# A third and a fourth pair of attention units as one group beside the first block of a fused attention and two-MLP kernel

## The chip, the cores and the metric

The kernel runs on one core of a Trainium2 chip. The metric is the device time in microseconds of one execution. Engines are named as the profile names them: PE (TensorE, matrix products), PEld (its weight loads), DVE (VectorE), ACT (ScalarE), POOL (GpSimd) and SP (the queue from which nearly all DMAs are issued).

## The reference

Local attention over 4 batches, 8 heads, 576 positions and head size 64 (window 32; in the upper four heads only every fourth position of a window of 128), then two MLPs over 2304 tokens with model width 512 and hidden width 2048, all in float32:

```
attn = softmax(where(mask, q @ k.T / sqrt(D), -1e9))
x = (attn @ v), heads side by side, as [2304, 512]
h = maximum(x @ w_in, 0);   x = (h * h) @ w_out        # first MLP
h = x @ w2_in;              out = (h * cos(h)) @ w2_out  # second MLP
```

## The kernel before, in words

The tokens are cut into five blocks of 512, 384, 512, 512 and 384 (`SIZES`). Each MLP goes through the blocks, and inside a block through 16 chunks of the hidden width. A chunk needs twelve matmuls in `product1` (L446, called h below: h9 is chunk 9 of block 0), elementwise work in `middle`, and twelve matmuls in `product2` (L499, called y), in two halves of six. Each product is made of three matmuls on operands that are split into a high and a low part, so every operand is split by ACT (high part) and DVE (low part) first. Weights are split by `split_w` (L144): DVE L152, L155, L158, ACT L161, DVE L163.

Attention is worked in units (one pair of heads, 192 positions). A number in `GROUPS` stands for two units, u and u+3, which here is called a pair. The first six pairs run before block 0. The later 18 are put beside the MLP by `group` (L386), in entries of one pair or of two. An entry of one or two pairs goes through these steps: scores on PE into two PSUM banks (L251); mask, maximum, exponential and normalisation on DVE and ACT (L398, L401, L335, L322, L323, L326); transposes on PE into one bank for each pair (L346) and ACT copies of them (L416); values on PE into two banks (L264); and `tokens_out` (L304), which drains these two banks: first every ACT copy (L313, the high part), then every DVE subtraction (L316, the low part), bank by bank, in as many pieces as the runs of tokens and the edges of blocks make.

The order of the work is written as events with a time. One unit of time is one hidden chunk, so block 0 is 0 to 16. In block 0, h of chunk fc stands at fc, and the two halves of y of chunk fc at fc + 2.5 and fc + 2.75. `PLACES` gives the time at which an entry's scores stand, and the values of the entry ahead of it stand 0.003 before that place, or 0.003 behind it where both entries hold one pair (`alone`, L604). Transposes come at the earlier of place + 1 + number of pairs and 0.5 before the next place (L605). The drain comes 0.12 behind the next place, or 0.42 where `alone` holds. Loads of queries and keys stand 1.5 before the place, loads of values 0.6 behind it.

From time 2.4 on each matmul is pinned behind the one written before it (`pe`, L207), so PE follows the order of the events exactly. For the other engines and for the loads the framework plans the order itself: the earliest event first among what is ready by its own costs.

Products h, scores, transposes and values all take their PSUM bank from one pool of four (`ps_h`, L105 and L212); the other four banks hold y. A buffer of the pool goes to its next user when the readers of the last one are done. Unit buffers in SBUF come from two rings of three, "uq" and "uv" (L188, L199); the second load of the second pair of an entry goes into the "uv" ring (L611).

```
        tr = min(t + 1 + len(us) + 0.5 * (i == 0), t2 - 0.5)
        in_steps([t, *soft, tr, later_by(tr, 0.1), t2 + (0.003 if alone else -0.003), later_by(t2, 0.42 if alone else 0.12)],
                 us, group, us)
```

Here t is the entry's place, t2 the next one, and soft holds the softmax steps, from 0.15 behind the place on.

Of the kernel before, what the change touches and what calls it, by code (L numbers as in the profile page):

```python
# [43 lines left out]
SQUARE_ON_ACT = (0, 4)  # L44
LAG = (2, 3)

GROUPS = ((12,), (13,), (18,), (19,), (20,), (14, 24), (30, 31), (32, 25), (26, 36), (42, 43), (44, 37), (38,))
PLACES = (3.74, 6.74, 8.74, 10.74, 12.74, 14.74, 22.49, 25.74, 28.74, 36.49, 42.74, 46.49, 51.74)
PINNED = (2.4, 96)


# [40 lines left out]
def attention_moe_moe(ctx: ExitStack, tc: tile.TileContext, units, windows, masks, w1, w2, out):  # L92
# [22 lines left out]
    def at(t, f, *a):  # L115
        events.append((t, len(events), f, a))
# [463 lines left out]
    at(before(49) - 1e-3, load_masks)  # L580
    place = PLACES
    with_weights = {us for us, t in zip(GROUPS, place) if t < NF}

# [14 lines left out]
    for t, n in MORE_FILL:  # L598
        at(before(t), fill_more, n)
    for i, us in enumerate(GROUPS):  # L600
        t, t2 = place[i:i + 2]
        by = lambda d: later_by(t, d)
        soft = [by(0.15)] + [by(d + a) for a in range(len(us)) for d in (0.75, 0.8)]
        alone = len(us) == 1 and len(GROUPS[min(i + 1, len(GROUPS) - 1)]) == 1  # L604
        tr = min(t + 1 + len(us) + 0.5 * (i == 0), t2 - 0.5)  # L605
# [148 lines left out]
```

## Time and profile before

| | |
|---|---|
| time, median of 3 runs | 859.26 us (859.16 to 860.20) |
| the profiled execution's own time | 859.97 us |
| its span, first to last instruction | 858.2 us |
| busy: PE, PEld, DVE, ACT, POOL | 850.1, 742.3, 499.1, 436.2, 52.8 us |
| mean granted TensorE clock | 0.999 |

Busy shares are means over the whole span. The matrix work of the two MLPs has the same shape from block to block, while the splitting of the first weights and the softmax of the later units lie in the first 130 us. What happens around the change is therefore read from the stretch of 70 to 130 us, in which block 0 ends.

### The profile page before, as it was taken

What the parts mean: (1) busy time and instruction counts of PE and PEld (TensorE: products, weight loads), DVE (VectorE), ACT (ScalarE), POOL (GpSimd) and SP (SyncE); (2) the same over time, 40 slices, a digit from 0 to 9 for tenths busy, and PEclk for the clock granted to TensorE, in tenths of its full rate; (3) what the DMA queues carried; (4) which work ended last, traced back from release to release, by engine and by line L of the source; (5) the groups of instructions that cost most, each with busy time, mean ns of one, the idle gap of its engine ahead of it and who ended that gap; (6) DMA issues with size and microseconds to landing.
All of it is one profiled execution on the core that took longest, in us unless ns stands there. A gap on an engine that the chain in (4) does not pass through costs nothing.

```text
span 858.2 us, 15509 instructions
## 1 busy us (share of the span) xinstructions
PE 850.1 (99%) x6251; PEld 742.3 (87%) x6251; DVE 499.1 (58%) x966; ACT 436.2 (51%) x1062; POOL 52.8 (6%) x86
## 2 busy tenths in 40 slices
PE   9899999999999999999999999999999999999998
PEld 5688889999888888889998888899988888888998
DVE  5999953464424342226999964556555555555554
ACT  6677873454424332225656654555544545445554
POOL 0000000000000000000002211111111111111110
PEclk9999999999999999999999999999999999999999
DMA  7867711240202020004565300010020002000101
GB/s 268 296 223 255 237 61 50 82 153 19 97 1 101 1 100 0 1 1 171 196 220 182 115 1 1 34 64 2 1 87 1 1 0 86 1 0 1 50 1 37
DMA packets 24663, 68.58 MB, mean 80 GB/s; under 512 B 2640, under 2 KB 8464, under 8 KB 24592
## 3 DMA queue, kind: packets, MB, share of 16 engines
q1 hardware_dynamic: 24432, 67.48, 22.8%
q8 instruction: 49, 0.80, 0.4%
q14 instruction: 22, 0.18, 0.1%
q10 hardware_dynamic: 160, 0.11, 0.0%
HBM read 58.15 MB, written 9.44 MB: 79 GB/s over the span
## 4 chain that ended last, share of the span: by engine, by line
PE 75%; DVE 10%; issue 8%; ACT 2%; DMA 2%; POOL 1%; SPq 0%; POOLq 0%; ACTq 0%; DVEq 0%
PE y L508 36%; PE h L452 35%; DVE wt L155 3%; DVE wt L158 2%; PE h L264 1%; DVE w L163 1%; DVE wt L152 1%; POOL kf L471 1%; DVE gl L494 1%; PE h L251 1%; DMA wraw<-w 1%; ACT early L335 1%; DMA early<-w 1%; PE h L346 1%; DMA xraw<-y 1%
## 5 line engine op out<-in xcount | busy, mean ns | idle before, releaser
L508 PE MATMUL y<-gh,w 128*128 128x512 f32 (+1 forms) x1280 | 397.1, 370 | 0.3 <-ACT o L526 0.3
L452 PE MATMUL h<-xh,w 128*128 128x512 f32 (+1 forms) x1280 | 393.2, 368 | 1.0 <-DVE w L163 1.0
L452 PEld LDWEIGHTS h<-xh,w 128*128 128x128 f32 x1280 | 237.4, 188 | 32.2 <-DVE w L163 1.4
L508 PEld LDWEIGHTS y<-gh,w 128*128 128x128 f32 x1280 | 237.6, 188 | 31.0 <-ACT o L526 0.6
L508 PE MATMUL y<-gl,w 128*128 128x512 f32 (+1 forms) x640 | 235.4, 368 | 0.2 <-DVE gl L494 0.2
L452 PE MATMUL h<-xl,w 128*128 128x512 f32 (+1 forms) x640 | 235.2, 367 | 0.0
L483 DVE TENSOR_TENSOR r<-h,r 128x512 f32<-128x512 f32 (+1 forms) x128 | 81.9, 640 | 168.6 <-ACT r L480 95.1
L494 DVE TENSOR_TENSOR gl<-r,gh 128x512 fp32r<-128x512 f32 (+1 forms) x160 | 101.9, 637 | 124.6 <-ACT gh L492 124.3
L492 ACT CAST gh<-r 128x512 fp32r<-128x512 f32 (+1 forms) x160 | 92.1, 576 | 89.7 <-PE y L508 74.6
L452 PEld LDWEIGHTS h<-xl,w 128*128 128x128 f32 x640 | 120.2, 188 | 15.3
L508 PEld LDWEIGHTS y<-gl,w 128*128 128x128 f32 x640 | 120.2, 188 | 15.0 <-DVE gl L494 0.6
L479 ACT ACTIVATE r<-r 128x512 f32<-128x512 f32 (+1 forms) x80 | 47.2, 590 | 142.1 <-DVE r L476 142.1
L471 POOL TENSOR_SCALAR kf<-kf 128x512 f32<-128x512 f32 (+1 forms) x80 | 52.1, 652 | 794.1 <-DVE wt L155 459.2
L464 ACT ACTIVATE r<-h 128x512 f32<-128x512 f32 (+1 forms) x80 | 44.2, 552 | 95.8 <-PE h L452 95.7
L470 ACT ACTIVATE kf<-h,magic 128x512 f32<-128x512 f32 (+1 forms) x80 | 51.0, 638 | 22.1 <-PE h L452 20.3
L480 ACT ACTIVATE r<-r,halfpi 128x512 f32<-128x512 f32 (+1 forms) x80 | 54.5, 681 | 2.5
L474 DVE SCALAR_TENSOR_TENSOR r<-kf,h 128x512 f32<-128x512 f32 (+1 forms) x80 | 50.0, 625 | 6.8 <-POOL kf L471 6.8
L476 DVE SCALAR_TENSOR_TENSOR r<-kf,r 128x512 f32<-128x512 f32 (+1 forms) x80 | 51.0, 638 | 2.4
L161 ACT CAST w<-wt 128x512 fp32r<-128x512 f32 x64 | 39.4, 620 | 24.1 <-DVE wt L158 24.1
L163 DVE TENSOR_TENSOR w<-wt,w 128x512 fp32r<-128x512 f32 x64 | 44.0, 694 | 4.0 <-ACT w L161 3.8
L335 ACT ACTIVATE p<-p,nm 128x64 f32<-128x64 f32 x108 | 36.2, 339 | 9.9 <-DVE nm L401 9.9
L155 DVE SCALAR_TENSOR_TENSOR wt<-wraw,wt 128x512 uint32<-128x512 uint32 x58 | 39.6, 686 | 0.7
(60 smaller groups left out, 392.9 us busy)
## 6 DMA issues: line engine op xcount, KB each, us to landing
wraw<-w SPq DMA_DIRECT2D x58, 512.0 KB, 4.0
uq<-units SPq DMA_DIRECT2D x36, 208.0 KB, 4.8
uv<-windows SPq DMA_DIRECT2D x18, 384.0 KB, 4.7
early<-w SPq DMA_DIRECT2D x6, 512.0 KB, 4.8
y<-o SPq DMA_DIRECT2D x6, 512.0 KB, 2.6
xraw<-y SPq DMA_DIRECT2D x6, 512.0 KB, 5.3
out<-o SPq DMA_DIRECT2D x6, 512.0 KB, 2.8
early<-units SPq DMA_DIRECT2D x6, 416.0 KB, 5.3
```

Source lines behind the costliest of these rows:

```text
L155: nc.vector.scalar_tensor_tensor(out=t, in0=high, scalar=0xC0000000, in1=t, op0=ALU.bitwise_and, op1=ALU.bitwise_or)
L163: nc.vector.tensor_tensor(out=lo, in0=f32(t), in1=f32(hi), op=ALU.subtract)
L452: pe(nc.tensor.matmul(h, w[:, c * P:(c + 1) * P], x[:, c, :], start=c == 0 and i == 0, stop=c == NC - 1 and i == 2))
L470: nc.scalar.activation(out=kf, in_=h, func=AF.Identity, bias=magic, scale=INV2PI)
L471: nc.gpsimd.tensor_scalar(out=kf, in0=kf, scalar1=-MAGIC, scalar2=1.0, op0=ALU.add, op1=ALU.mult)
L474: nc.vector.scalar_tensor_tensor(out=r, in0=kf, scalar=-C1, in1=h, op0=ALU.mult, op1=ALU.add)
L476: nc.vector.scalar_tensor_tensor(out=r, in0=kf, scalar=-C2, in1=r, op0=ALU.mult, op1=ALU.add)
L480: nc.scalar.activation(out=r, in_=r, func=AF.Sin, bias=halfpi, scale=-1.0)
L483: nc.vector.tensor_tensor(out=r, in0=h, in1=r, op=ALU.mult)
L492: nc.scalar.copy(out=gh, in_=r)
L494: nc.vector.tensor_tensor(out=gl, in0=r, in1=f32(gh), op=ALU.subtract)
L508: pe(nc.tensor.matmul(y[e], w[:, e * P:(e + 1) * P], g, start=fc == 0 and n == 0, stop=fc == NF - 1 and n == 2,))
```

## The change

```diff
-GROUPS = ((12,), (13,), (18,), (19,), (20,), (14, 24), (30, 31), (32, 25), (26, 36), (42, 43), (44, 37), (38,))
-PLACES = (3.74, 6.74, 8.74, 10.74, 12.74, 14.74, 22.49, 25.74, 28.74, 36.49, 42.74, 46.49, 51.74)
+GROUPS = ((12,), (13,), (18, 19), (20,), (14, 24), (30, 31), (32, 25), (26, 36), (42, 43), (44, 37), (38,))
+PLACES = (3.74, 6.74, 8.99, 11.99, 14.49, 22.49, 25.74, 28.74, 36.49, 42.74, 46.49, 51.74)
```

The entries (18,) and (19,), at 8.74 and 10.74, become one entry (18, 19) at 8.99. Entry (20,) goes from 12.74 to 11.99, and (14, 24) from 14.74 to 14.49. All else that hangs on places follows. The order on PE is now: transposes of 13 at 8.49; values of 13 at 8.987 and scores of 18 and 19 at 8.99; h9 at 9; transposes of 18 and 19 at 11.49; their values at 11.987 and scores of 20 at 11.99; h12 at 12; transposes of 20 at 13.99; its values at 14.487 and scores of 14 and 24 at 14.49. The drain of 13 goes from 9.16 to 9.11, that of 18 (and 19) to 12.11, that of 20 from 14.86 to 14.61. In the places before, at x.74, six matmuls of y stood between a place and the next h.

## Rows read from the trace of the kernel before

**Rows 1.** The page: busy time of the engine, share of the span.

```profile
...
PE 850.1 (99%) x6251; PEld 742.3 (87%) x6251; DVE 499.1 (58%) x966; ACT 436.2 (51%) x1062; POOL 52.8 (6%) x86
...
```

**Rows 2.** Waits of PE, 40 to 850 us: total, times, longest.

```profile
...
PE y L508 <- ACT o L526: 0.3, 1, 0.3
```

**Rows 3.** Waits of all engines, 60 to 126 us.

```profile
...
PEld h L452 <- DVE p L398: 0.5, 1, 0.5
...
```

**Rows 4.** Timeline of PE, 71 to 79 us: start, duration, line, count.

```profile
...
74.29 0.40 PE L508 MATMUL y<-gh,w 128*128 128x512 f32 x1
74.61 0.76 PE L251 MATMUL h<-uq 64*32 64x64 f32 x48
75.30 0.90 PE L264 MATMUL h<-pts,uv 64*64 64x32 f32 x48
76.13 0.50 PE L508 MATMUL y<-gh,w 128*128 128x512 f32 x1
76.46 0.40 PE L508 MATMUL y<-gl,w 128*128 128x512 f32 x1
...
77.39 0.40 PE L508 MATMUL y<-gh,w 128*128 128x512 f32 x1
77.84 0.50 PE L452 MATMUL h<-xh,w 128*128 128x512 f32 x1
...
```

**Rows 5.** Timeline of DVE, 75 to 100 us.

```profile
...
77.43 0.61 DVE L398 SCALAR_TENSOR_TENSOR p<-h,given 128x192 f32<-128x192 f32 x2
77.96 0.42 DVE L152 TENSOR_SCALAR wt<-wraw 128x512 uint32<-128x512 uint32 x1
78.30 0.55 DVE L401 TENSOR_REDUCE nm<-p 128x6 f32<-128x384 f32 x1
78.76 0.69 DVE L155 SCALAR_TENSOR_TENSOR wt<-wraw,wt 128x512 uint32<-128x512 uint32 x1
...
81.16 0.74 DVE L316 TENSOR_TENSOR xl<-h,xh 128x128 fp32r<-128x128 f32 x4
...
98.61 0.68 DVE L494 TENSOR_TENSOR gl<-r,gh 128x512 fp32r<-128x512 f32 x1
...
```

**Rows 6.** Timeline of PE, 112 to 123 us.

```profile
...
112.12 0.49 PE L346 MATMUL h<-ident,p 128*128 128x128 f32 x3
112.37 0.48 PE L508 MATMUL y<-gh,w 128*128 128x512 f32 x1
...
114.77 1.27 PE L251 MATMUL h<-uq 64*32 64x64 f32 x96
115.97 0.50 PE L508 MATMUL y<-gh,w 128*128 128x512 f32 x1
...
```

**Rows 7.** Timeline of PE, 130.9 to 133 us.

```profile
...
131.28 0.82 PE L346 MATMUL h<-ident,p 128*128 128x128 f32 x6
131.85 0.48 PE L508 MATMUL y<-gh,w 128*128 128x512 f32 x1
...
```

**Rows 8.** Timeline of PE, 168 to 174 us.

```profile
...
169.29 1.60 PE L264 MATMUL h<-p,uv 64*64 64x32 f32 x96
...
```

**Rows 9.** Timeline of ACT, 75 to 79 us; the brackets hold the idle time before and its releaser.

```profile
...
76.23 0.67 ACT L313 CAST xh<-h 128x128 fp32r<-128x128 f32 x4 [0.33 <-PE h L264]
...
```

**Rows 10.** Timeline of ACT, 111 to 119 us.

```profile
...
114.87 0.91 ACT L313 CAST xh<-h 128x48 fp32r<-128x48 f32 x6 [1.05 <-PE h L264]
...
```

**Rows 11.** Timeline of DVE, 112 to 120 us.

```profile
...
115.43 1.14 DVE L316 TENSOR_TENSOR xl<-h,xh 128x48 fp32r<-128x48 f32 x6 [2.61 <-ACT xh L313]
...
```

**Rows 12.** Timeline of ACT, 120 to 128 us.

```profile
...
125.76 1.54 ACT L326 ACTIVATE p<-p,rs 128x64 f32<-128x64 f32 x6
...
```

**Rows 13.** Timeline of the SP queue, 40 to 106 us: DMA issues.

```profile
...
78.86 0.33 SPq L202 DMA_DIRECT2D uv<-windows  x1
...
```

**Rows 14.** Timeline of PE, 29 to 33 us.

```profile
...
31.43 0.73 PE L452 MATMUL h<-xh,w 128*128 128x512 f32 x2 [0.96 <-DVE w L163]
...
```

**Rows 15.** Stretches: length, busy time of each engine, granted clock (PEclk), DMA share.

```profile
...
30.00:34.00 4.00, 3.04 (x13) 2.18 (x13) 3.90 (x11) 1.37 (x5) 0.00 (x0) 1.00 1.00 365
...
```

## The prediction

> **What bounds the kernel now.** I read the page first: PE is busy for 850.1 of 858.2 us [rows 1], so time is won or lost only where PE does more, does less, or stands still. Next the waits. From 40 us on PE has a single wait that counts as idle, 0.3 us [rows 2]; so a microsecond of stall that the change puts on PE is not won back later, as no later stall is there to shrink. Then the stretch of the change. The view of waits shows one that PE's busy time hides: PE's weight load for h waited for DVE's masking of scores, L398, for 0.5 us [rows 3]. On PE's timeline the last y before it starts at 77.39 and h9 at 77.84 [rows 4], 0.45 apart where two matmuls of this shape are 0.23 apart (76.46 to 77.39 are four steps). DVE's timeline says why: the first of the two L398 ends near 77.78 (start 77.43, half of 0.61 plus the overlap) [rows 5]. This is the bank pool at work: the scores of 18 and the values of 13 had taken all four banks, and h9 had to wait until one was read out. The last view is DVE itself: from 75 to 100 us it has no idle time worth naming, and the planner's order puts work behind work with earlier event times. The drain of 13 (event 9.16) ran at 81.16 [rows 5] though its ACT copies were done at 76.90 [rows 9]; splits and L494 with events up to 9.05 went first. Its neighbours 12, 18 and 19 were drained at the same point of the order.
>
> **What goes.** Attention costs PE its own time and a toll at each change of form: 0.09 going in (74.29 to 74.61 is 0.32, less 0.23) and 0.10 going out (76.13 to 76.46) [rows 4]. Scores of one pair take 0.69 and values 0.83 [rows 4]; scores of two pairs 1.20 [rows 6]; values of two pairs 1.53 (1.60 less the 0.07 by which the single one's duration passes its step) [rows 8]; transposes 0.25 for one pair [rows 6] and 0.57 for two [rows 7], with 0.08 going out in both.
>
> - Before, places 8.74 to 14.74: four tolls 0.76, scores 3 x 0.69 + 1.20 = 3.27, values 4 x 0.83 = 3.32, three transposes 3 x 0.33 = 0.99; sum 8.34.
> - After, places 8.99 to 14.49: three tolls 0.57, scores 1.20 + 0.69 + 1.20 = 3.09, values 0.83 + 1.53 + 0.83 = 3.19, transposes 0.65 + 0.33 = 0.98; sum 7.83.
>
> That saves 0.51. The stall of 77.84 goes too: 0.22 and the slow restart of 0.10, together 0.32. In all 0.83 less.
>
> **What comes: h9 directly behind the place.** Before, six y stood between a place and the next h. At 8.99 none does. Values of 13 and scores of 18 and 19 take all four banks, and h9 needs one at once. The first to come free is the first bank of the values, after two ACT copies and two DVE subtractions. Queued behind h9 on PE is everything, since matmuls are pinned.
>
> - PE: as before up to 74.29; then the second half of y, six steps of 0.23, and the toll: values from 75.98 to 76.81, scores to 78.01. Then h9 could start.
> - DVE: as before up to 77.43. From there to the drain at 81.16 it spent 3.73, of which L398 and L401 of the scores took 0.53 (77.43 to 77.96) and 0.46 (78.30 to 78.76) [rows 5]. These now have the event 9.14, behind the drain at 9.11, so they drop out: the drain starts at 77.43 + 2.74 = 80.17. Two of its four pieces are half of 0.74 [rows 5], so the bank is free at 80.55 and h9 starts at 80.6, after the 0.06 that lay between L398's end and h9 before.
>
> First stall: 80.6 - 78.0 = 2.6. From below 0: had DVE taken the two pieces when their copies end (76.9 plus half of 0.67 [rows 9], plus 0.4), the bank would be free at 77.7, ahead of PE. From above 3.8: two more split steps of 0.6 in front. I take 2.6, as the order of four drains out of four speaks for it.
>
> **The same at 11.99.** From h9 at 80.6 PE has six blocks of twelve matmuls (12 x 0.227 = 2.72), a restart of 0.10, transposes 0.65, and the toll: values of 18 and 19 from 97.8 to 99.3, scores of 20 to 100.0. Then h12 stands. The first bank holds six pieces now (18 and 19 follow one another in a dilated head, so their runs of tokens join: six, where three and four stood before). The copies start 0.1 behind the values, at 99.4, and six take 0.91 [rows 10], to 100.3; six subtractions take 1.14 [rows 11], to 101.4. DVE itself gets there in time: before, it needed 99.3 (98.61 + 0.68) - 81.16 = 18.1 from one drain to this point of the order [rows 5]; now one drain of 18 less (1.1) and its mask and maximum more (1.0), so it is there at about 98.2. Second stall 1.4. From below 0.5, if the subtractions run with the copies and scores cover a little more; from above 2.6, if DVE lags as at 8.99.
>
> A rule that speaks against the change is weighed here. The first subtraction of six pieces started at 115.43, 0.56 behind the first copy [rows 10, 11], which is about when the third copy, the last of its bank, ends. The Trainium skill, "PSUM — Partial Sum Buffer", section on bank collisions, says that two engines must not access one bank and quadrant at once, reads included, so copies and subtractions of one bank can only follow one another; by that rule the second stall stays at 1.4, and if piece followed piece it would be about 0.9. The row agrees with the rule.
>
> **What costs nothing, and its cover.** At 14.49 both halves of y of chunk 12 follow, 2.72 us, and scores 1.20, against a drain of about 2: no stall; DVE is idle 2.61 before that drain already [rows 11]. Were that cover gone it would cost as much as the second stall. The transposes of 18 and 19 at 11.49 need the last normalisation, L326. For the pair of pairs (14, 24) this ran at 125.76 to 127.30 [rows 12], 11.3 us behind the end of its scores at 115.97, with DVE free. Here there are 94.3 - 78.0 = 16.3 us, with DVE full; I take 0, bounded by 2. Loads: unit 22 goes into the "uv" ring at 7.79 and takes the third buffer, which is free from the start; 18's and 19's values then wait for the buffers of 12 and 13, the last free at 76.8; a load of values issued at 78.86 [rows 13] shows when such a buffer is taken again, and that is 19 us ahead of 97.8, when PE reads it. SP works in order, so such a load held up would hold weight loads behind it; as DVE never starves, up to 1 us, taken as 0. ACT and DVE lose two drain pieces each for good, beside PE: 0.
>
> **Sum.** -0.83 + 2.6 + 1.4 = +3.2. On the profiled execution, 859.97 (span 858.2 and 1.8 around it), that is 863.2. It stands 0.7 over the median, so the forecast by the median is 859.26 + 3.2 = 862.4.
>
> **Rivals.**
> 1. *No change: the drains are prompt.* If the planner puts the two subtractions of 13 where their copies end, the first stall is 0 and the second stays 0.5 to 1.4: -0.3 to +0.6, so 859.0 to 859.9. It decides from a first stall below 1.2 on. For it: L398 slipped between split steps at 77.43. Against: that had the earlier event; a drain never did so.
> 2. *Faster: h finds a bank.* If at one of the two places a bank outside the group's is free, both stalls go: 859.26 - 0.83 = 858.4. Against: four banks and four users.
> 3. *More stalls.* The last normalisation or SP's order delays the transposes by 1 to 2, or DVE lags at 11.99 too: 863.4 to 865. For it: DVE is full to 100 us.
> 4. *The clock falls.* PE stood still for 0.96 at 31.43 [rows 14] and the granted clock of 30 to 34 us stayed at 1.00 [rows 15]; 2.6 in one piece occurs in no stretch of this trace. If it fell from 2.4 to 1.2 GHz, the next twelve matmuls would take twice 2.72: +2.7, 865.1. The Trainium skill, "TensorE: Matmul & The Clock Gate", part 1, says that "the default state is throttled, and activity releases the throttle"; no row here shows the lower level after a pause.
>
> **How the numbers follow.** Forecast 57%, its own range 861.2 to 863.4; rival 1 21%, rival 2 5%, rival 3 12%, rival 4 5%. The range 859.5 to 864.4 leaves out rivals 2 and 4, half of rival 1 and the far end of rival 3. What a measurement can tell from no change is 0.2%, 1.7 us. Slower holds the forecast and rivals 3 and 4, less the forecast's low end where the first stall is half of what I take: 70%. Same holds rival 1 and that low end: 24%. Faster 6%.
>
> **What would show it.** PE (or PEld) h L452 waiting for DVE xl L316 twice, near 78 to 80.6 and 100 to 101.5; L316 starting near 80.2, right behind L494; L398 behind it; scores x96 between 76.8 and 78.0. No wait on L316, or two far below 1 us in sum, makes the forecast wrong; so does a wait at L346 for L326 larger than either.

## The result and the profile after

The changed kernel takes 866.60 us in the median of four runs (865.32 to 867.21), the kernel before 859.69 on the same chip: a ratio of 1.0077 (95% interval 1.0065 to 1.0089), 6.9 us slower. The forecast was slower by 3.2, with a range up to 864.4. The profiled execution took 867.21, with a span of 865.4 against 858.2.

The waits of PE over the whole execution (waiting engine, line, releaser: total, times, longest) hold the two waits that were forecast, and they are the largest:

```profile
PE h L452 <- DVE xl L316: 4.4, 2, 2.4
PE e L346 <- DVE xl L316: 1.7, 3, 0.8
```

PE's timeline around the first place, in the same columns as [rows 4]; the bracket holds the idle time and its releaser:

```profile
...
75.74 0.90 PE L264 MATMUL h<-pts,uv 64*64 64x32 f32 x48
76.57 1.49 PE L251 MATMUL h<-uq 64*32 64x64 f32 x96
80.49 0.47 PE L452 MATMUL h<-xh,w 128*128 128x512 f32 x1 [2.43 <-DVE xl L316]
...
81.72 0.63 PE L452 MATMUL h<-xl,w 128*128 128x512 f32 x1
...
84.91 0.40 PE L508 MATMUL y<-gh,w 128*128 128x512 f32 x1
```

By their length in [rows 6] the scores would end at 76.57 + 1.20 = 77.77, and h9 starts at 80.49: a stall of 2.7. The bracket has 2.43 of it, as the scores took 1.49 here in place of 1.27 [rows 6]; a short pause ahead of their last four matmuls, which comes back in the last section, changes nothing while h9 waits for the drain anyway. What is new stands behind the stall. From 81.72 on matmuls are 0.43 apart where they were 0.23 [rows 4], and h9's twelve take 4.42 to the first y at 84.91, where 2.82 was expected. The stretches (length, busy times, then the granted clock as the third value from the end) say why:

```profile
77.80:80.40 2.60, 0.26 (x5) 0.11 (x4) 2.60 (x7) 0.75 (x4) 0.00 (x0) 1.00 0.88 264
80.40:81.20 0.80, 0.71 (x3) 0.66 (x4) 0.80 (x5) 0.26 (x1) 0.00 (x0) 1.00 1.04 396
81.25:84.60 3.35, 3.35 (x9) 2.64 (x8) 3.35 (x8) 1.10 (x6) 0.00 (x0) 0.50 0.97 364
84.70:95.00 10.30, 10.30 (x47) 8.50 (x46) 8.09 (x18) 9.67 (x34) 0.00 (x0) 1.00 0.52 178
102.20:104.20 2.00, 0.05 (x4) 0.03 (x1) 2.00 (x10) 1.47 (x11) 0.00 (x0) 1.00 0.88 253
105.15:108.50 3.35, 3.35 (x9) 2.57 (x9) 3.28 (x8) 0.00 (x0) 0.00 (x0) 0.50 0.75 260
```

After each stall the granted clock is 0.50, 1.2 GHz in place of 2.4, for some eight or nine matmuls. While PE stood still DVE was busy without a break (2.60 of 2.60, 2.00 of 2.00), and its timeline around the first stall shows what it did, to be held against [rows 5]:

```profile
77.17 0.43 DVE L152 TENSOR_SCALAR wt<-wraw 128x512 uint32<-128x512 uint32 x1
77.51 0.69 DVE L494 TENSOR_TENSOR gl<-r,gh 128x512 fp32r<-128x512 f32 x1
78.11 0.69 DVE L155 SCALAR_TENSOR_TENSOR wt<-wraw,wt 128x512 uint32<-128x512 uint32 x1
78.72 0.69 DVE L163 TENSOR_TENSOR w<-wt,w 128x512 fp32r<-128x512 f32 x1
79.32 0.69 DVE L158 SCALAR_TENSOR_TENSOR wt<-wraw,wt 128x512 uint32<-128x512 uint32 x1
79.92 0.75 DVE L316 TENSOR_TENSOR xl<-h,xh 128x128 fp32r<-128x128 f32 x4
80.58 0.88 DVE L398 SCALAR_TENSOR_TENSOR p<-h,given 128x192 f32<-128x192 f32 x3
```

Five operations that nobody on PE was waiting for, then the drain, with the mask behind it. Around the second place, PE's timeline holds the second stall and a smaller wait ahead of it, in the six transposes, which took 0.57 in [rows 7]:

```profile
95.83 1.43 PE L346 MATMUL h<-ident,p 128*128 128x128 f32 x6
97.02 0.48 PE L508 MATMUL y<-gh,w 128*128 128x512 f32 x1
...
99.97 1.60 PE L264 MATMUL h<-p,uv 64*64 64x32 f32 x96
101.50 0.76 PE L251 MATMUL h<-uq 64*32 64x64 f32 x48
104.20 0.47 PE L452 MATMUL h<-xh,w 128*128 128x512 f32 x1 [1.95 <-DVE xl L316]
```

The transposes take 1.19, a wait of 0.6 for the last normalisation. DVE's load alone does not explain it. DVE stood idle for 2.1 ahead of 87.25, waiting for exponentials, and half of these ran on ACT behind L464, which waited 2.05 for the late and slow h9:

```profile
85.11 0.60 ACT L464 ACTIVATE r<-h 128x512 f32<-128x512 f32 x1 [2.05 <-PE h L452]
87.25 0.17 DVE L322 TENSOR_SCALAR rs<-sm 128x6 f32<-128x6 f32 x1 [2.12 <-ACT p L335]
```

Scores end at 102.19 and h12 starts at 104.20: a stall of 2.0. DVE and ACT between, which answer to [rows 10, 11]:

```profile
102.33 0.68 DVE L158 SCALAR_TENSOR_TENSOR wt<-wraw,wt 128x512 uint32<-128x512 uint32 x1
102.93 2.17 DVE L316 TENSOR_TENSOR xl<-h,xh 128x80 fp32r<-128x80 f32 x12
```

```profile
101.60 1.60 ACT L313 CAST xh<-h 128x80 fp32r<-128x80 f32 x12 [0.86 <-PE h L264]
```

Half of the twelve copies, those of the first bank, end about 102.5; DVE was then in a split step that the planner had put ahead, and began the drain at 102.93.

So the account is: PE's own time and the old stall -0.8, first stall +2.7, transposes +0.6, second stall +2.0, and twice 1.6 for the lower clock, +3.2: together +7.7, against 7.2 by the spans. PE reached the transposes of 13 at 72.56 in place of 72.71, which is 0.15 of the difference; and 0.2 is won back near 555 us, where the kernel before has its one wait of [rows 2] and the changed kernel has none.

### The profile page after: what moved, and what is told of

Same layout as the page of the kernel before. It is cut to its first block, busy times and chain, and to the rows that moved or that the text cites. A ratio compares the mean times of both kernels' runs of the same rounds, so it can differ in the third digit from the quotient of the medians.

```text
span 865.4 us, 15498 instructions
## 1 busy us (share of the span) xinstructions
PE 852.2 (98%) x6245; PEld 744.8 (86%) x6251; DVE 500.2 (58%) x964; ACT 435.4 (50%) x1060; POOL 52.8 (6%) x86
## 4 chain that ended last, share of the span: by engine, by line
PE 73%; DVE 12%; issue 9%; ACT 3%; DMA 2%; POOL 1%; SPq 0%; POOLq 0%; ACTq 0%; DVEq 0%
PE y L508 35%; PE h L452 35%; DVE wt L155 3%; DVE wt L158 2%; DVE w L163 2%; DVE wt L152 1%; PE h L264 1%; DVE gl L494 1%; POOL kf L471 1%; PE h L251 1%; ACT early L335 1%; DMA early<-w 1%; PE h L346 1%; DMA xraw<-y 1%; DVE xl L316 1%
## 5 line engine op out<-in xcount | busy, mean ns | idle before, releaser
L494 DVE TENSOR_TENSOR gl<-r,gh 128x512 fp32r<-128x512 f32 (+1 forms) x160 | 101.9, 637 | 124.5 <-ACT gh L492 124.1
L464 ACT ACTIVATE r<-h 128x512 f32<-128x512 f32 (+1 forms) x80 | 44.2, 552 | 104.5 <-PE h L452 104.4
```

The source lines that it names most:

```text
L494: nc.vector.tensor_tensor(out=gl, in0=r, in1=f32(gh), op=ALU.subtract)
```

## The experiments

Times are medians; each is set against the kernel before on the same chip in the same set of runs (859.96 in the first set of four, 859.87 in the second, 860.08 in the last two).

**Place moved back, grouping kept.** Is it the grouping or where it stands?

```diff
-PLACES = (3.74, 6.74, 8.99, 11.99, 14.49, ...
+PLACES = (3.74, 6.74, 8.74, 11.74, 14.49, ...
```

> The grouping of the change kept, the places moved back by 0.25 so that six y stand between place and next h (8.74, 11.74, 14.49). Theory (h waits for the first drained bank, and DVE takes the drain only at its event's turn): the drain's events are now 8.86 and 11.86, ahead of the splits at 8.93 to 9.05, so the stalls of h9 and h12 go to 0 to 0.3 each, the clock stays at 1.00, and the transposes at 11.24 may wait about 1 for the last normalisation: 859 to 861 us. Rival (a group of two pairs is itself too much beside block 0): 864 or more.

860.32, ratio 1.0001 (0.9992 to 1.0010). The waits on L316 shrink from 4.4 to one of 0.5, the transposes do not wait, the clock stays at 1.00. The grouping itself does no harm that can be told from noise. It does not win its 0.8 either: beside the 0.5 of that wait, a new pause of 0.6 stands behind the 144 small matmuls at the first place, one that is put down to no engine:

```profile
76.14 0.50 PE L508 MATMUL y<-gh,w 128*128 128x512 f32 x1
76.47 0.40 PE L508 MATMUL y<-gl,w 128*128 128x512 f32 x1
77.51 0.51 PE L508 MATMUL y<-gh,w 128*128 128x512 f32 x1 [0.64 <-issue]
```

**More cover at the second place.**

```diff
-PLACES = (3.74, 6.74, 8.99, 11.99, 14.49, ...
+PLACES = (3.74, 6.74, 8.74, 12.24, 14.74, ...
```

> The grouping kept, places 8.74, 12.24 and 14.74: six y behind the first place, twelve behind the second, transposes at 11.74. Theory: no stall at either h, a wait at the transposes of 0 to 0.6, clock 1.00: 858.7 to 859.8 us, the same as the kernel before or a little below (0.5 of PE's own time and the old 0.3 stall saved). Rival (the grouping costs): 862 or more.

860.23, ratio 1.0000 (0.9992 to 1.0009). No wait of PE on L316 or L326 is left from 70 us on, but the pause of 0.7 is there again, nearly as long as the saving. The time is 0.4 above the forecast range. What it is without the pause, the last experiment shows.

**The order of DVE alone.** PE's order is that of the changed kernel.

```diff
-        in_steps([t, *soft, tr, ..., later_by(t2, 0.42 if alone else 0.12)],
+        in_steps([t, *soft, tr, ..., later_by(t2, 0.42 if alone else 0.001 if t2 in (8.99, 11.99) else 0.12)],
```

> The change with its order on PE untouched; only the event of the two drains goes from 0.12 to 0.001 behind the place (8.991 and 11.991), ahead of the splits and L494 at 9.05 and 12.05 in DVE's order. Theory (the drain's turn on DVE sets the stall): first stall from 2.7 to about 0.9, second from 2.0 to about 1.2, so the clock falls at most once: 861 to 863.5 us. Rival (missing cover alone sets the stall, whatever DVE's order): 866.6 us as the changed kernel.

865.14, ratio 1.0053 (1.0040 to 1.0066). The first stall goes as forecast, from 2.7 to 0.9, with nothing changed but the drain's turn (the first bank's ACT copies were done before 77.4 in both kernels):

```profile
76.89 1.45 PE L251 MATMUL h<-uq 64*32 64x64 f32 x96
79.00 0.47 PE L452 MATMUL h<-xh,w 128*128 128x512 f32 x1 [0.66 <-DVE xl L316]
```

So missing cover alone does not set it; DVE's order does. Behind this shorter stall the clock stays at 1.00, and PE reaches the transposes 3.1 sooner than in the changed kernel. But 1.2 of that comes back at once, as the softmax is not ready:

```profile
92.71 0.49 PE L346 MATMUL h<-ident,p 128*128 128x128 f32 x3
94.01 0.33 PE L346 MATMUL h<-ident,p 128*128 128x128 f32 x1 [0.81 <-ACT p L326]
...
95.05 0.48 PE L508 MATMUL y<-gh,w 128*128 128x512 f32 x1
```

They take 2.34 in place of 1.19. The second stall did not shrink (2.4), against my 1.2, and the clock falls behind it: the first bank's copies were done near 100.5, yet DVE's drain came at 101.33, behind two more split steps. The forecast of 861 to 863.5 missed for these two reasons.

**The bank alone.** DVE's order at the first place and its number of operations are those of the changed kernel, but the two drains read the copied part in SBUF, so that the bank is free without DVE. The low part of the tokens of 13, 18 and 19 is left out (zero).

```diff
-            nc.vector.tensor_tensor(out=xl, in0=piece, in1=f32(xh), op=ALU.subtract)
+            nc.vector.tensor_tensor(out=xl, in0=f32(xh) if us in ((13,), (18, 19)) else piece, in1=f32(xh), op=ALU.subtract)
```

> The change with its order on PE and DVE; the subtractions of the two drains read the copied part in SBUF in place of the bank (the low part of these tokens is left out, it becomes zero), so that a bank is free when ACT's copies end, while DVE does as many operations as before. Theory (h waits for the bank that DVE has not read yet): first stall 0, second about 0.2, no fall of the clock behind them; DVE is as far behind as before, so the transposes of 18 and 19 wait 1.5 to 2.5 for the softmax: 860.5 to 863.5 us. Rival (h waits for DVE work in some other way, or missing cover alone sets it): 866 us, with the same two waits.

863.70, ratio 1.0037 (1.0024 to 1.0050). The drain still runs at 79.86, but h9 starts at 77.98, so it was the bank and nothing else of DVE's that h waited for:

```profile
77.98 0.50 PE L452 MATMUL h<-xh,w 128*128 128x512 f32 x1
79.86 0.76 DVE L316 TENSOR_TENSOR xl<-xh 128x128 fp32r<-128x128 f32 x4
```

The softmax is late instead (2.6 at the transposes), and h12 waits 0.3 for ACT's copies:

```profile
91.74 0.49 PE L346 MATMUL h<-ident,p 128*128 128x128 f32 x3
93.89 0.33 PE L346 MATMUL h<-ident,p 128*128 128x128 f32 x1 [1.66 <-ACT p L326]
...
94.93 0.47 PE L508 MATMUL y<-gh,w 128*128 128x512 f32 x1
```

The eight runs part by their mean granted clock: three at 0.999 or 1.000 took 860.95 to 861.52, five at 0.997 or 0.998 took 863.28 to 864.46. The trace is of one of the three (861.52); in the five the clock fell somewhere, against the forecast of no fall, and where is not known.

**One place at a time.**

```diff
-PLACES = (3.74, 6.74, 8.99, 11.99, 14.49, ...
+PLACES = (3.74, 6.74, 8.99, 12.24, 14.74, ...   # the first alone
+PLACES = (3.74, 6.74, 8.74, 11.99, 14.49, ...   # the second alone
```

> Grouping kept, only the first of the two bad places: 8.99, then 12.24 and 14.74 (twelve y behind the second). Theory (each place directly before an h costs its own stall and, behind it, a stretch at 1.2 GHz): first stall 2.7, one stretch of 3.4 us at the lower clock (about 1.6), no second stall, transposes with no wait; -0.8 + 2.7 + 1.6 - 0.3: 862.5 to 864 us. Rival (the loss comes from the second place, or only from both together): below 861 us.

> Grouping kept, only the second of the two bad places: 8.74, then 11.99 and 14.49. Theory: no wait for the drain at h9 (but the 0.8 us in which PE waits for nothing shown, as in the two kernels with 8.74), second stall about 2.0 to 3 (PE reaches it earlier, DVE does not), one stretch at the lower clock: 862.5 to 864.5 us. Rival (the first place alone makes the loss): 860 to 861 us.

863.02, ratio 1.0048 (1.0033 to 1.0062), and 863.32, ratio 1.0043 (1.0028 to 1.0058). Both lie inside their forecasts. Each has one wait on L316 (2.1 and 2.2 of idle time) and one stretch at the lower clock; the two excesses over the kernel before, 3.15 and 3.45, add up to 6.6, nearly the 6.9 of both.

**The place without the grouping.** The kernel before, with its single pairs:

```diff
-PLACES = (3.74, 6.74, 8.74, 10.74, 12.74, 14.74, ...
+PLACES = (3.74, 6.74, 8.99, 10.99, 12.99, 14.74, ...
```

> The grouping undone, the move kept: the five single pairs of the kernel before, with places 8.99, 10.99 and 12.99 directly before an h. Theory (the place, not the grouping): h9, h11 and h13 wait for the first bank that DVE reads, about 2.7, 1.5 to 2.5 and 0.5 to 1.5 us, with a stretch at the lower clock behind the longer ones: 865 to 870 us. Rival (the group of two pairs makes the loss): 859 to 861 us.

866.67, ratio 1.0080 (1.0065 to 1.0095): as bad as the change, with three places directly before an h where the change has two. Singles have their scores first, so h waits for the mask that reads the scores' bank, and the three waits sum to 3.9 with 2.9 the longest:

```profile
PE h L452 <- DVE p L398: 3.9, 3, 2.9
```

The time is inside the forecast, but not by its parts: the second and third wait are 0.8 and 0.2, below what was expected, and the clock falls once, for twice as long as in the changed kernel.

**PE kept at work in the stalls.** 11 and 8 matmuls with zero weights into a y bank, in the changed kernel, and then 11 in the kernel with the first place alone.

```diff
+    zero = const.tile([P, P], BF16, name="zero")
...
+    def keep_busy(n):
+        for _ in range(n):
+            pe(nc.tensor.matmul(ys[0, 0][0], zero, given[:, P:P + 512], start=False, stop=False))
...
+        nc.vector.memset(zero, 0.0)
...
+    at(8.995, keep_busy, 11)
+    at(11.995, keep_busy, 8)      # not in the second of the two kernels
```

> The change as it is, with 11 matmuls of zeros that add nothing to a y bank put ahead of h9 and 8 ahead of h12, so that PE works while it would stand still (about 2.4 and 1.7 us of stalls of 2.7 and 2.0). Theory (some 3 us of the loss are the lower clock that follows the two stalls): the granted clock stays at 1.00 and the time falls by about 3, to 863.0 to 864.0 us. Rival (the clock is a companion, the loss lies elsewhere): within 0.5 of the changed kernel's 866.6 us.

867.51 (866.20 to 871.83), ratio 1.0092 (1.0072 to 1.0113): neither forecast. The clock of the profiled execution (866.41) held at 1.00 through both places. From h9 to the transposes of (14, 24) PE took 54.55, where the changed kernel took 56.85, so 2.3 were saved by then (lines of this kernel stand five lower: L457 is h, L513 y, L321 the drain, L351 the transposes):

```profile
79.97 0.47 PE L457 MATMUL h<-xh,w 128*128 128x512 f32 x1
134.52 0.82 PE L351 MATMUL h<-ident,p 128*128 128x128 f32 x6
```

In the changed kernel the second of these is

```profile
137.34 0.82 PE L346 MATMUL h<-ident,p 128*128 128x128 f32 x6
```

Yet the time is no lower: near 194 and 235 us PE pauses 0.87 and 1.03 for "issue", in spots where the changed kernel does not. The wait for the drain at h12 is still there too, as the zeros cover only a part of it:

```profile
PE y L513 <- issue: 1.9, 2, 1.0
PE h L457 <- DVE xl L321: 1.4, 1, 1.4
```

> The kernel with only the first bad place (8.99, 12.24, 14.74), with the 11 matmuls of zeros ahead of h9. Theory (the stall makes the clock fall, and the stretch at 1.2 GHz costs 1.6 of the 3.2 us of this place): the granted clock stays at 1.00 behind the stall, h9 starts at the same time, and the time goes from 863.0 to 861.0 to 862.0 us, unless the 22 instructions more bring a new pause in which PE waits for nothing shown, as they did with both places. Rival (the clock costs nothing in the end, since DVE sets the pace to 100 us): 862.5 to 863.5 us.

862.69, ratio 1.0033 (1.0021 to 1.0044): inside the rival's forecast, not the theory's. The excess over the kernel before is 2.6, against 3.15 without the zeros, and the two intervals overlap. The clock held in the profiled execution, and the mean clock was 0.999 or 1.000 in seven of the eight runs, against 0.995 to 0.998 in all five without the zeros: it falls because PE stands still. What that saves, the traces show in part. From h9 to the transposes of (14, 24) the kernel with the zeros takes 53.13, the one without 54.00, which is 0.9 less of the 1.6 that the slow stretch takes:

```profile
81.40 0.58 PE L457 MATMUL h<-xh,w 128*128 128x512 f32 x1
134.53 0.82 PE L351 MATMUL h<-ident,p 128*128 128x128 f32 x6
```

```profile
80.34 0.47 PE L452 MATMUL h<-xh,w 128*128 128x512 f32 x1 [2.06 <-DVE xl L316]
134.34 0.81 PE L346 MATMUL h<-ident,p 128*128 128x128 f32 x6
```

But h9 starts 1.1 later here, and not at the same time as the theory wanted: PE was already behind by 0.4 at 40 us, and DVE comes to the drain 0.9 later. So this does not settle what a slow stretch costs in the end.

**Without the pause.** The kernel with 8.74, 12.24 and 14.74, with eight of the matmuls that warm PE early on left out:

```diff
-FILL = (7, 3, 2, 4, 4, 6)
-MORE_FILL = ((18.63, 3),)
+FILL = (7, 3, 2, 2, 2, 3)
+MORE_FILL = ((18.63, 2),)
```

> The kernel with places 8.74, 12.24 and 14.74 (860.2, as the kernel before), with eight warming matmuls fewer in the early part, so that PE's instruction stream stands 16 instructions earlier. Theory (the 0.8 us pause behind the 144 small matmuls at 8.74 is a fetch of instructions that was asked for inside them): the pause is gone, 859.3 to 859.7 us, a little under the kernel before. Rival (the pause belongs to the place itself, or the missing matmuls cost the clock early): 860 us or more.

860.46, ratio 1.0006 (0.9997 to 1.0015): the time is the rival's, though the pause behind the small matmuls is gone, as the theory had it. PE gets to h12 sooner and now waits there 0.56 for L316, and more goes at two waits of 0.3 and 0.6 near 470 and 555 us, for L494 and L526.

```profile
102.33 0.39 PE L508 MATMUL y<-gh,w 128*128 128x512 f32 x1
103.28 0.47 PE L452 MATMUL h<-xh,w 128*128 128x512 f32 x1 [0.56 <-DVE xl L316]
```

No version of the grouping beat the kernel before.

## Why the prediction was right and where it was wrong

- **What bounds, and that nothing wins time back later:** right for the whole (PE was 7.5 behind the kernel before at the end of block 0, and 7.2 at the end). Inside block 0 it was not: the DVE-bound part up to about 100 us gives a saved stall back at the next wait, as the drain's turn, the bank alone and the kernel without the pause showed.
- **h9 waits for the first drained bank, because of the drain's turn on DVE:** right. 2.7 for 2.6, the drain at 79.92 for 80.17, the mask behind it. That it is the bank, and that it is the turn, were each shown by changing that alone.
- **h12:** the mechanism right, the size 2.0 for 1.4. The term that failed is "DVE itself gets there in time": it did, but the planner had put split steps with later events ahead of it (it seems that by its own costs the copies were not done yet), and one of them held the drain 0.4 past their end. The Trainium skill, "PSUM — Partial Sum Buffer", section on bank collisions, says that two engines must not access one bank and quadrant at once, reads included. The changed kernel agrees where DVE was free: at 121.83 the first subtraction begins right behind the third copy, the last of its bank, which ends at 121.80.
- **Transposes at 11.49 at nothing:** 0.6, within the bound of 2. The margin left out ACT's turn: L464 waited for the late h9 with half of the exponentials behind it, and DVE, taken as full, stood idle for 2.1. With the 0.6 more at h12 this is rival 3 in small.
- **PE's own time:** right; values and scores of one pair take what the rows said, and so do the transposes where nothing holds them (0.57 with the places moved back).
- **The clock stays (rival 4, 5%):** this step failed and cost most of the miss. The chance was read from one pause of 0.96 [rows 14, 15], and a second fall was not thought of; the price of one fall was put at 2.7. The clock fell behind both stalls at 1.6 each, and these 3.2 are most of the 4.0 by which the profiled execution passed the forecast; the rest is 0.6 at the transposes and 0.6 at h12, less what PE was ahead at the start and won back late. The first stall was longer than any pause that [rows 14] shows, so no row spoke for the clock's staying, and rival 4 should have been part of the forecast. The Trainium skill, "TensorE: Matmul & The Clock Gate", part 1, has the default throttled and activity releasing it. The runs agree as far as they go: the clock fell behind stalls of 2 us and more, and held where zeros kept PE at work.

What stays open: how much of the 3.2 would be saved in the end if the clock held. The zeros saved 2.3 of 3.2 in one kernel and 0.9 of 1.6 in another up to 134 us, each with pauses of its own. Runs of one kernel point the same way. The changed kernel took 865.32 in its one run at a mean granted clock of 0.998, and 866.47 to 867.21 in the three at 0.996; the kernel with the drains moved took 863.52 in its one run at 1.000, and 864.66 to 866.02 in the five at 0.998. By estimate 0.002 of the mean is one stretch of 3.4 us at half the clock (1.7 of 865). But only one run of each kernel was traced, so that these runs differ in the clock alone is not shown.

## What to carry to other kernels

Before moving work to just ahead of a product, count the PSUM banks it takes and ask which reader must free the next one, and at which turn of that reader's queue: six matmuls of cover took a stall of 2.7 us to nothing, and 0.1 of a time step in a priority took it to 0.9. A stall on PE that is longer than any the trace has shown should be priced with the lower clock behind it. Where another engine is full, a wait taken away from PE appears at the next thing that engine owes it, so look for what is late next before counting a gain.

## What the runs showed of the hardware

- From 40 us on the granted clock fell to 0.50 at six idle times of PE: 2.43 and 1.95 in the changed kernel, 2.32 with the drains moved, 2.06 with the first place alone, 2.25 with the second alone, 2.87 with the single pairs. It did not fall behind 0.66 and 0.81 (drains moved), 0.84 (single pairs), 1.37 (zeros at both places) and 1.66 (the bank alone). The point of the fall differs. In the changed kernel it was less than 1 us behind the point at which PE had begun to work again (81.2 for 80.49, 105.1 for 104.20), with the drains moved at that point (102.6), and with the single pairs 1.2 ahead of it (79.0 for 80.24), still in the pause. There the lower level held for 6.8 us in place of 3.4, and h9's twelve matmuls took 5.3 (80.24 to 85.53) where 2.8 was expected for the changed kernel, so that this one fall cost 2.5 and not 1.6:

```profile
78.00:79.00 1.00, 0.00 (x0) 0.00 (x0) 1.00 (x3) 0.39 (x3) 0.00 (x0) 1.00 0.95 238
79.10:85.70 6.60, 5.46 (x13) 4.30 (x14) 5.72 (x17) 2.72 (x13) 0.00 (x0) 0.50 0.68 235
```

- PE can pause for nothing that the profile names, by 0.2 to 1.0 us, among long runs of small matmuls or shortly behind them: with the place at 8.74 in the third y behind 144 of them, with the place at 8.99 ahead of the last four scores, and near 194 and 235 us in the kernel with both sets of zeros. At the first place the spot is the same in the traces of all nine kernels that have the group there with all the warming matmuls: ahead of PE's 1112th weight load, be it one of a y or of a score (0.2 to 0.3 in four of them, of which the changed kernel is one). With eight warming matmuls fewer, 16 instructions, this load is one of h9's, and there is no pause. So it hangs on where PE's stream of instructions stands. The Trainium skill, "Runtime: NRT & Kernel Launch", section on instruction fetch mechanics, says that instructions are fetched in blocks of 16 KiB (256 instructions) while earlier ones run, at a cost that is mostly hidden. The page of the kernel before shows an instruction queue, q8, with 49 packets and 0.80 MB, 16 KB each, which agrees; by estimate from the 256 of that section, 49 blocks hold 12544 instructions, and PE's matmuls and weight loads on that page are 12502. That these pauses are such fetches was inferred, not seen, and hidden they were not.
